# QKV row 4 turned by a transposing DMA, with row 3's turn and row 1's evictions rearranged

## The chip, the cores and the metric

The kernel runs on one core of one Trainium2 chip. The metric is the device time of one execution in microseconds; lower is better. The engines named below are TensorE (PE in the profile: matmuls, and PEld for its weight loads), VectorE (DVE), ScalarE (ACT), GpSimd (POOL) and SyncE (SP, which here only issues DMAs).

## What is computed

The input x has 2048 tokens of 576 numbers in bfloat16. A layer norm without weights gives xn. Two branches start from xn, and their sum goes onto x: local attention with 32 heads of 18, where each token looks at 8 earlier positions with a stride of 2, and a gated feed-forward block of width 4608.

```python
def _A_ref(x, wqkv, wo):
    H = 32; Dh = D // H
    W, dil = 8, 2
    qkv = (x @ wqkv).reshape(B, S, 3, H, Dh).transpose(2, 0, 3, 1, 4)
    q, k, v = qkv[0], qkv[1], qkv[2]
    idx = arange(S)[:, None] - (arange(W) * dil)[None, :]
    ...
    logits = jnp.einsum("bhsd,bhswd->bhsw", q, kg) * Dh ** -0.5
    logits = jnp.where(mask[None, None, :, :], logits, -1e9)
    attn = _softmax(logits, axis=-1)
    o = jnp.einsum("bhsw,bhswd->bhsd", attn, vg)
    return o.transpose(0, 2, 1, 3).reshape(B, S, D) @ wo
def _B_ref(x, w_gate, w_up, w_down):
    return (_silu(x @ w_gate) * (x @ w_up)) @ w_down
xn = _layernorm(x, axis=-1)
return x + _A_ref(xn, A_wqkv, A_wo) + _B_ref(xn, B_w_gate, B_w_up, B_w_down)
```

## The kernel before

**Rows and tiles.** The 2048 tokens are 16 "rows" of 128 tokens. Token 16p + r lies in partition p of row r. A row of xn has 576 columns and is padded to 640, so that it turns into five K tiles of 128. The last K tile holds columns 512 to 575 twice, in partitions 0 to 63 and 64 to 127.

**Stages.** First comes the QKV stage: each of the 16 rows is normalized, turned (its transposed form goes into `xnT`, since a matmul wants the contracted dimension in the partitions), multiplied by `wqkv` and evicted from PSUM. It ends near 59 us. Then follow four passes over 512 tokens each, with the feed-forward block on TensorE and the attention on VectorE beside it. The change lies in the first rows of the QKV stage.

**Order.** The schedule is written by hand: each engine gets its instructions in the order of the program text, and semaphores hold an instruction until its inputs are there. SP issues its DMAs in program order, and waits at each one for what it needs before it goes on to the next. PSUM has eight banks, which the pool `ps` deals in turn.

**A row on TensorE** (`p_row`, L321). The columns of the product are in four groups of 432, one PSUM bank each (`t[0]` to `t[3]`). The contraction is cut in halves of 64 partitions, and two matmuls, one for each half, run beside each other for two different groups: such a pair is the unit of the row. A row has 18 pairs: ten with `swap` 0 and eight with `swap` 1, where the halves change groups. Between the two a fence runs through a GpSimd no-operation (`fence_after`, L313), so GpSimd must be free when it is due. `between` is called after one K tile of `swap` 1, given by `at` as (pair of groups, K tile); there the next row is turned. Row 1 has its first K tile multiplied ahead (`u`).

**Turning a row.** Rows 0 and 1 are turned by `transp_pe`; rows 2, 3 and 4 by `transp_halves` (L274): ten matmuls of 64x64 against the identity, in five pairs, into two banks `pt`, which ScalarE and VectorE copy into `xnT` (L287). Rows from 5 on are turned by a transposing DMA from SP (`transp_dma`, L289), straight from the normalized row into `xnT`. Row 0 goes through `transp_dma` as well, but only for a use after the QKV stage.

**Normalizing a row.** `ln_stats` takes two halves of statistics (L214) and aggregates them (L218) on VectorE; `ln_sqrt` (L229) is on ScalarE; `normalize` (L467) takes the reciprocal (L234), applies it (L240) and fills the padding, for rows 0 and 1 with a GpSimd operation (L243) that reads the input, for the others with a VectorE copy (L246) of what L240 wrote. `ln_open(c)` makes the small tiles for rows 4c to 4c + 3.

**Evicting a row** (`p_evac`, L345). Six parts; `dve` lists those on VectorE, the others are on ScalarE. Parts 1 and 2 read `t[2]`, 3 and 4 read `t[1]`, part 0 reads `t[0]` and part 5 `t[3]`.

**DMAs of the stretch.** SP has issued by then, in this order, the inputs, the first gate and up weights (`load_gu(0)`), row 0's transposing DMA and two small fills of zeros (`wz`) into the rings `Kr` and `Vr`, 14 pieces of 1152 bytes each, all into partition 0. Rows 5 and later follow.

Of the kernel before, what the change touches and what calls it, by code (L numbers as in the profile page):

```python
# [70 lines left out]
def kernel(  # L71
# [124 lines left out]
    def new_ps(name):  # L196
        return ps.tile([P, 512], f32, name=name, tag="ps")
# [4 lines left out]
    def ln_open(c):  # L202
        mv = lns.tile([P, 4, 2], f32, name="mv")
        rstd = lns.tile([P, 4], f32, name="rstd")
        ln[c] = (xc_b[c], xn_b[c % 2], mv, rstd)
# [3 lines left out]
    def ln_half(r, k):  # L209
        c, j = divmod(r, 4)  # L210
        xc, xn, mv, rstd = ln[c]
        if k == 0:
            sums[r] = lns.tile([P, 2, 6], f32, name="stats")
        nc.vector.bn_stats(sums[r][:, k, :], xc[:, j, k * HALF:(k + 1) * HALF])  # L214

    def ln_aggr(r):
        c, j = divmod(r, 4)
        nc.vector.bn_aggr(ln[c][2][:, j, :], sums[r][:].rearrange("p c s -> p (c s)"))  # L218

    def ln_stats(r, n=1):  # L220
        for i in range(r, r + n):
            ln_half(i, 0)
            ln_half(i, 1)
            ln_aggr(i)

    def ln_sqrt(r, n=1):
        c, j = divmod(r, 4)
        xc, xn, mv, rstd = ln[c]
        nc.scalar.activation(rstd[:, j:j + n], mv[:, j:j + n, 1], ACT.Sqrt, bias=eps_t[:], scale=1.0)  # L229

    def ln_recip(r, n=1):
        c, j = divmod(r, 4)
        rstd = ln[c][3]
        nc.vector.reciprocal(rstd[:, j:j + n], rstd[:, j:j + n])  # L234

    def ln_apply(r):
        c, j = divmod(r, 4)
        xc, xn, mv, rstd = ln[c]
        dst = xn[:, j] if r else xn0
        nc.vector.tensor_scalar(dst[:, 0:D], xc[:, j], mv[:, j, 0:1], rstd[:, j:j + 1],  # L240
                                op0=ALU.subtract, op1=ALU.mult)
        if r < 2:
            nc.gpsimd.tensor_scalar(dst[:, D:DPAD], xc[:, j, 512:D], mv[:, j, 0:1], rstd[:, j:j + 1],  # L243
                                    op0=ALU.subtract, op1=ALU.mult)
        else:
            nc.vector.tensor_copy(dst[:, D:DPAD], dst[:, 512:D])  # L246
# [27 lines left out]
    def transp_halves(r):  # L274


        c, j = divmod(r, 4)
        xn = ln[c][1]
        pt = [new_ps("pt") for half in range(2)]
        for kt in range(KT):  # L280
            for half in range(2):
                rows = slice(64 * half, 64 * half + 64)
                nc.tensor.matmul(pt[half][:, kt * 64:(kt + 1) * 64], xn[rows, j, kt * P:(kt + 1) * P],  # L283
                                 ident[rows, rows], start=True, stop=True)
        for half, eng in enumerate((nc.scalar.copy, nc.vector.tensor_copy)):
            lo = r * P + 64 * half
            eng(xnT[:, :, lo:lo + 64], pt[half][:, 0:KT * 64].rearrange("p (k t) -> p k t", t=64))  # L287

    def transp_dma(r):  # L289
        c, j = divmod(r, 4)  # L290
        nc.sync.dma_start_transpose(xnT[:, :, r * P:(r + 1) * P], ln[c][1][:, j, :] if r else xn0)
# [7 lines left out]
    def p_mm(t, g, kt, half, r, start, stop):  # L299
        rows = slice(0, P) if half is None else slice(64 * half, 64 * half + 64)  # L300
        return nc.tensor.matmul(t[g][:, 0:G], xT_of(r)[rows, kt, :], w_at(g, kt, rows),  # L301
                                start=start, stop=stop)
# [10 lines left out]
    def fence_after(mm):  # L313
        f = nc.gpsimd.engine_nop()
        tc.add_manual_dep(f.ins, mm.ins.name, SYNC, reason="first half done")
        return f

    def fence_before(mm, f):
        tc.add_manual_dep(mm.ins, f.ins.name, SYNC, reason="banks change row tiles")

    def p_row(r, between=None, at=(0, 1), t=None):  # L321


        done = t is not None
        t = t or [None] * NG
        fence = {}
        for swap in range(2):
            for i in range(2):
                for kt in (0, 1, 2, 3) if swap else (0, 4, 1, 2, 3):
                    if done and kt == 0:  # L330
                        continue
                    for half in range(2):
                        g = i + 2 * (half ^ swap)
                        if t[g] is None:
                            t[g] = new_ps("qkv_ps")
                        mm = p_mm(t, g, kt, half, r, swap == 0 and kt == 0, swap == 1 and kt == 3)
                        if swap == 0 and kt == 3 and half == 1:
                            fence[i] = fence_after(mm)
                        if swap and kt == (1 if done else 0) and half == 0:
                            fence_before(mm, fence[i])  # L340
                    if swap and (i, kt) == at and between is not None:
                        between()
        return t

    def p_evac(r, t, only=range(6), between=None, last=6, dve=(5,)):  # L345


        c, j = divmod(r, 4)
        ks, vs = stage[2 * c % 4], stage[(2 * c + 1) % 4]
        vdst = vs[:, j, :].rearrange("p (d h) -> p d h", h=H)  # L350
        parts = [
            (QO[:, r, 0:G], t[0][:, 0:G]),
            (ks[:, j, HALF:D], t[2][:, 0:HALF]),
            (vdst[:, :, 0:8], t[2][:, HALF:G].rearrange("p (h d) -> p d h", d=DH)),
            (QO[:, r, G:D], t[1][:, 0:D - G]),
            (ks[:, j, 0:HALF], t[1][:, D - G:G]),
            (vdst[:, :, 8:H], t[3][:, 0:G].rearrange("p (h d) -> p d h", d=DH)),
        ]
        for n in only:
            if n == last:  # L360
                between()
            if r:
                (nc.vector.tensor_copy if n in dve else nc.scalar.copy)(*parts[n])  # L363
            elif n in dve:
                nc.vector.tensor_scalar(*parts[n], ln[0][3][:, 0:1], None, op0=ALU.mult)
            else:
                nc.scalar.mul(*parts[n], ln[0][3][:, 0:1])
# [24 lines left out]
    dve = Filler()  # L392
# [74 lines left out]
    def normalize(r, n=1):  # L467
        ln_recip(r, n)
        for i in range(r, r + n):
            ln_apply(i)  # L470
            if i > 4:
                transp_dma(i)

    def turn(r):
        return lambda: transp_halves(r)
# [15 lines left out]
    copy_pt(nc.scalar.copy, 0, (3, 4), pb[:, 2 * P:])  # L491
    ln_recip(0)
    ln_apply(0)
    ln_recip(1)
    ln_apply(1)

    t = [new_ps("qkv_ps") for g in range(NG)]
# [10 lines left out]
    u = [None] * NG  # L508
# [5 lines left out]
    ln_stats(2)  # L514
    ln_sqrt(2)
    normalize(2)
    p_evac(0, t, (5, 0, 3, 2, 4, 1), dve=(5, 2))
    ln_half(3, 0)
# [3 lines left out]

    p_row(1, turn(2), (0, 1), u)
    ln_aggr(3)
    p_evac(1, u, (0, 1, 2), dve=(1, 2))
    ln_sqrt(3)
    p_evac(1, u, (3, 4, 5), dve=())
    normalize(3)
    ln_open(1)
    ln_stats(4)  # L530
    for ring in (Kr, Vr):
        nc.sync.dma_start(ring[0:1, 0:HALO, :], wz[0:1, :].unsqueeze(1).to_broadcast([1, HALO, D]))

    t = p_row(2, turn(3))
    ln_stats(5)
    p_evac(2, t, (0, 1, 2), dve=())
    ln_sqrt(4, 2)
    p_evac(2, t, (3, 4, 5), dve=())
    normalize(4, 2)

    t = p_row(3, turn(4))
    ln_stats(6)
    p_evac(3, t, range(6), lambda: ln_sqrt(6), 4, ())
    normalize(6)
# [7 lines left out]
    for r in range(4, R):  # L552
        t = p_row(r)
# [92 lines left out]
    for tt in range(NTT):  # L646
# [28 lines left out]
        for sub in range(0, RT, 2):  # L675
            t, fence = {}, {}
# [36 lines left out]
```

## Time and profile before

| what | us |
|---|---|
| median of 3 runs | 503.44 (503.23 to 503.55) |
| the profiled execution, its own time | 503.32 |
| its span, first to last instruction | 501.5 |
| TensorE busy | 496.8 |
| VectorE busy | 329.0 |
| ScalarE busy | 200.6 |
| GpSimd busy | 2.6 |

The profile is of one execution. The span is what lies between its first and its last instruction; the time is 1.8 us longer. Times in the trace are counted from the start of the span. In lines of the order of time the first number is the start, the second the duration, then come the engine, the line, the operation, and what it writes and reads. SPq is SP issuing a DMA; "to landing" is the time from the start of the issue to the last completion. Several equal instructions in a row are merged into one line with their count, so the duration of such a line runs from the first start to the last end. Matmul durations overlap, since they are pipelined; what a matmul costs is seen from the start of the next one.

### The profile page before, as it was taken

How to read it: one execution, taken by the hardware profiler on the slowest of the kernel's cores; microseconds unless marked ns; L12 is line 12 of the kernel's file. 1: busy time of each engine (PE TensorE's matmuls, PEld its weight loads, DVE VectorE, ACT ScalarE, POOL GpSimd, SP SyncE). 2: the span in 40 equal slices, each digit the busy share in tenths (PEclk: the TensorE clock that was granted, in tenths of full speed). 3: DMA queues.
4: the chain of work that ended last, by engine and by line, in shares of the span. 5: the costliest groups of instructions: out<-in, count | busy, mean ns of one | idle time of the engine just before them, and what ended most of it. 6: DMA issues, size and time to landing. Idle time of an engine off the chain costs nothing.

```text
span 501.5 us, 13267 instructions
## 1 busy us (share of the span) xinstructions
PE 496.8 (99%) x5795; PEld 282.8 (56%) x5795; DVE 329.0 (66%) x478; ACT 200.6 (40%) x415; POOL 2.6 (1%) x9
## 2 busy tenths in 40 slices
PE   8999999999999999999999999999999999999997
PEld 4555544444677644444777544445777444446775
DVE  5889597998999698999897139995980222221001
ACT  4756657645300255544300445557000454553000
POOL 2000000000000000000000000000000000000000
PEclk9999999999999999999999999999999999999999
DMA  8689989898731045535631154453700335442200
GB/s 322 164 207 228 320 268 294 260 318 272 186 114 61 25 147 185 190 112 174 166 106 47 30 182 154 131 189 110 181 26 14 106 110 177 159 126 39 76 14 25
DMA packets 77186, 75.42 MB, mean 150 GB/s; under 512 B 22708, under 2 KB 72528, under 8 KB 77128
## 3 DMA queue, kind: packets, MB, share of 16 engines
q1 hardware_dynamic: 76840, 73.98, 49.2%
q8 instruction: 45, 0.74, 0.7%
q10 hardware_dynamic: 288, 0.59, 0.3%
q14 instruction: 13, 0.11, 0.1%
HBM read 58.76 MB, written 5.90 MB: 129 GB/s over the span
## 4 chain that ended last, share of the span: by engine, by line
PE 98%; DMA 1%; DVE 0%; SPq 0%; issue 0%
PE g_ps L600 56%; PE d_ps L629 32%; PE qkv_ps L301 11%; DMA hT<-in_A_wqkv_dram 1%; DVE ot L643 0%; PE pt L283 0%; SPq L145 0%; PE pt L262 0%; PE warm_ps L262 0%
## 5 line engine op out<-in xcount | busy, mean ns | idle before, releaser
L600 PE MATMUL g_ps<-xnT,gu 64*128 64x512 bf16 x2592 | 280.4, 376 | 0.0
L600 PEld LDWEIGHTS <-gu 64*128 64x128 bf16 x2592 | 126.1, 94 | 152.9
L611 ACT ACTIVATE sg<-g_ps 128x512 bf16<-128x512 f32 x144 | 87.3, 606 | 156.6 <-PE g_ps L600 156.6
L629 PE MATMUL d_ps<-wd,hT 64*128 64x288 bf16 x2304 | 146.4, 283 | 0.0
L629 PEld LDWEIGHTS <-hT 64*128 64x128 bf16 x2304 | 112.2, 94 | 29.7
L613 DVE TENSOR_TENSOR hT<-sg,uc 128x512 bf16<-128x512 bf16 x144 | 60.0, 419 | 93.9 <-ACT uc L612 93.8
L612 ACT CAST uc<-g_ps 128x512 bf16<-128x512 f32 x144 | 85.2, 592 | 0.0
L414 DVE TENSOR_REDUCE PP<-PP 128x64 f32<-128x1152 bf16 x64 | 84.9, 1346 | 0.4
L301 PE MATMUL qkv_ps<-hT,xnT 64*128 64x432 bf16 (+1 forms) x536 | 50.1, 343 | 0.0
L409 DVE TENSOR_TENSOR PP<-QO,Kr 128x2304 bf16<-128x2304 bf16 (+1 forms) x35 | 43.5, 1249 | 7.0 <-DMA Kr<-hT 6.8
L641 DVE TENSOR_TENSOR ot<-d_ps,xr 128x288 bf16<-128x288 f32 x30 | 12.3, 450 | 51.1 <-PE d_ps L629 51.1
L441 DVE TENSOR_TENSOR PP<-Vr,A 128x2304 bf16<-128x2304 bf16 (+1 forms) x35 | 43.2, 1250 | 0.4
L301 PEld LDWEIGHTS <-xnT 64*128 64x128 bf16 (+1 forms) x536 | 25.9, 94 | 22.5 <-ACT xnT L287 0.2
L446 DVE TENSOR_TENSOR PP<-PP 128x2304 bf16<-128x2304 bf16 x24 | 32.5, 1353 | 0.3
L611 ACT ACT_TABLE_LOAD x5 | 6.4, 1283 | 47.2 <-PE g_ps L600 47.2
L629 PE MATMUL d_ps<-wo,xnT 64*128 64x288 bf16 x288 | 22.9, 283 | 0.0
L363 ACT CAST hT<-qkv_ps 128x288 bf16<-128x288 f32 (+2 forms) x58 | 21.1, 427 | 0.5 <-ACT hT L363 0.5
L434 ACT ACTIVATE PP<-PP 128x1024 f32<-128x1024 f32 x4 | 4.2, 1056 | 31.2 <-DVE PP L430 31.2
L629 PEld LDWEIGHTS <-xnT 64*128 64x128 bf16 x288 | 14.0, 94 | 3.6
L643 ACT CAST ot<-d_ps 128x288 bf16<-128x288 f32 x1 | 0.4, 399 | 38.8 <-PE d_ps L629 38.8
L363 ACT CAST QO<-qkv_ps 128x432 bf16<-128x432 f32 (+1 forms) x30 | 12.3, 409 | 7.4 <-PE qkv_ps L301 7.4
L214 DVE BATCH_NORM_STATS2 stats<-wd 128x6 f32<-128x288 bf16 x32 | 12.9, 444 | 2.8 <-DMA wd<-in_A_x_dram 2.6
(53 smaller groups left out, 89.4 us busy)
## 6 DMA issues: line engine op xcount, KB each, us to landing
gu<-in_B_w_gate_dram SPq DMA_DIRECT2D x36, 512.0 KB, 3.9
gu<-in_B_w_up_dram SPq DMA_DIRECT2D x36, 512.0 KB, 5.2
wd<-in_B_w_down_dram SPq DMA_DIRECT2D x9, 576.0 KB, 6.4
kv_d<-hT SPq DMA_DIRECT2D x5, 576.0 KB, 6.0
gu<-in_B_w_gate_dram SPq DMA_DIRECT2D x36, 64.0 KB, 5.0
gu<-in_B_w_up_dram SPq DMA_DIRECT2D x36, 64.0 KB, 4.6
xr<-in_A_x_dram SPq DMA_DIRECT2D x8, 288.0 KB, 3.9
out_dram<-ot SPq DMA_DIRECT2D x16, 144.0 KB, 1.8
```

The source lines that it names most:

```text
L214: nc.vector.bn_stats(sums[r][:, k, :], xc[:, j, k * HALF:(k + 1) * HALF])
L301: return nc.tensor.matmul(t[g][:, 0:G], xT_of(r)[rows, kt, :], w_at(g, kt, rows), start=start, stop=stop)
L363: (nc.vector.tensor_copy if n in dve else nc.scalar.copy)(*parts[n])
L409: nc.vector.tensor_tensor(prod[:, a:b], QO[:, RT * tt + a:RT * tt + b, :], Kr[:, s:s + b - a, :], op=ALU.mult)
L414: nc.vector.tensor_reduce(L[:, w, rs], prod[:, rs].rearrange("p r (h d) -> p r h d", d=DH), axis=AX.X, op=ALU.add)
L441: nc.vector.tensor_tensor(dst[:, a:b], Vr[:, s:s + b - a, :].rearrange("p r (d h) -> p r d h", h=H), A[:, w, a:b].unsqueeze(2).to_broadcas ...
L446: nc.vector.tensor_tensor(dst, acc, pv, op=ALU.add)
L600: mm = nc.tensor.matmul(ring_ps[j][b][:], gu[rows, slot, k, fc], xnT[rows, kt, tok], start=(swap == 0 and kt == 0), stop=(swap == 1 and kt ...
L611: nc.scalar.activation(sg[:], t[0][:], ACT.Silu)
L612: nc.scalar.copy(uc[:], t[1][:])
L613: nc.vector.tensor_tensor(hT[:, ch * FC + j, :], sg[:], uc[:], op=ALU.mult)
L629: mm = nc.tensor.matmul(t[sub][h][:, 0:HALF], a[rows], w[rows, h * HALF:(h + 1) * HALF], start=(swap == 0 and n == 0), stop=(swap == 1 and ...
```

## The change

Row 4's turn on TensorE goes; `normalize(4)` issues a transposing DMA instead, as for the later rows. Row 4 is normalized alone and sooner: `ln_open(1)` and the first half of its statistics stand before row 1's evictions, the second half, the aggregate and the root behind `normalize(3)`, and `normalize(4)` right behind row 2's matmuls. Its padding is filled by GpSimd. Row 1's parts 1 and 2 are evicted by ScalarE, behind row 3's root. Row 3 is turned after K tile 0 of `swap` 1 of row 2, where it was K tile 1. Row 5 is then normalized alone too, with its root after part 3 of row 2's evictions.

```diff
@@ ln_apply
-        if r < 2:
+        if r in (0, 1, 4):
             nc.gpsimd.tensor_scalar(dst[:, D:DPAD], xc[:, j, 512:D], mv[:, j, 0:1], rstd[:, j:j + 1],
                                     op0=ALU.subtract, op1=ALU.mult)
@@ normalize
             ln_apply(i)
-            if i > 4:
+            if i > 3:
                 transp_dma(i)
@@ the first rows
     p_row(1, turn(2), (0, 1), u)
     ln_aggr(3)
-    p_evac(1, u, (0, 1, 2), dve=(1, 2))
+    ln_open(1)
+    ln_half(4, 0)
+    p_evac(1, u, (0,), dve=())
     ln_sqrt(3)
-    p_evac(1, u, (3, 4, 5), dve=())
+    p_evac(1, u, (2, 1, 3, 4, 5), dve=())
     normalize(3)
-    ln_open(1)
-    ln_stats(4)
+    ln_half(4, 1)
+    ln_aggr(4)
+    ln_sqrt(4)
     for ring in (Kr, Vr):
         nc.sync.dma_start(ring[0:1, 0:HALO, :], wz[0:1, :].unsqueeze(1).to_broadcast([1, HALO, D]))
 
-    t = p_row(2, turn(3))
+    t = p_row(2, turn(3), (0, 0))
+    normalize(4)
     ln_stats(5)
-    p_evac(2, t, (0, 1, 2), dve=())
-    ln_sqrt(4, 2)
-    p_evac(2, t, (3, 4, 5), dve=())
-    normalize(4, 2)
-
-    t = p_row(3, turn(4))
+    p_evac(2, t, (0, 1, 2, 3), dve=())
+    ln_sqrt(5)
+    p_evac(2, t, (4, 5), dve=())
+    normalize(5)
+
+    t = p_row(3)
     ln_stats(6)
     p_evac(3, t, range(6), lambda: ln_sqrt(6), 4, ())
     normalize(6)
```

## The prediction

> **What bounds the kernel now.** I read the page first, then what TensorE waits for, then the stretch from 10 to 24 us in order of time, then the DMA share by stretch and the landing times of single transposing DMAs. The page, its shares, chain and queues:
>
> ```profile
> span 501.5 us, 13267 instructions
> ...
> PE 496.8 (99%) x5795; PEld 282.8 (56%) x5795; DVE 329.0 (66%) x478; ACT 200.6 (40%) x415; POOL 2.6 (1%) x9
> ...
> q8 instruction: 45, 0.74, 0.7%
> ...
> PE 98%; DMA 1%; DVE 0%; SPq 0%; issue 0%
> ```
>
> All waits of TensorE over the whole span:
>
> ```profile
> PE warm_ps L174 <- PEq L697: 0.8, 1, 0.8
> PE pt L262 <- DVE wd L251: 0.7, 1, 0.7
> ```
>
> TensorE is the chain, and its only waits are over by 5.2 us. In the trace its matmuls then follow each other without a hole from 10.1 us to 498.1 us. So a microsecond is gained only by taking work from TensorE, and any new wait on it is paid in full. The stretch of the change, in order of time (start, duration, engine):
>
> ```profile
> 7.26 0.64 POOL L243 TENSOR_SCALAR wd<-wd,mv,rstd 128x64 bf16<-128x64 bf16 x1
> ...
> 11.35 1.44 SPq L291 DMA_TRANSPOSE xnT<-A  x1
> ...
> 12.84 1.03 SPq L532 DMA_DIRECT2D Kr<-ot  x1
> ...
> 13.91 0.82 SPq L532 DMA_DIRECT2D Vr<-ot  x1
> ...
> 15.40 0.31 PE L283 MATMUL pt<-ident,wd 64*128 64x64 bf16 x10
> ...
> 18.84 0.31 PE L283 MATMUL pt<-ident,wd 64*128 64x64 bf16 x10
> ...
> 18.98 21.33 PE L301 MATMUL qkv_ps<-hT,xnT 64*128 64x432 bf16 x232
> 19.03 6.25 SPq L291 DMA_TRANSPOSE xnT<-wd  x3
> ```
>
> DMA share (next to last column) by stretch:
>
> ```profile
> 13.30:17.80 4.50, 4.50 (x62) 2.46 (x60) 3.65 (x13) 3.13 (x12) 0.00 (x0) 1.00 1.13 313
> 17.80:20.10 2.30, 2.30 (x38) 1.28 (x36) 2.01 (x7) 1.58 (x5) 0.00 (x0) 1.00 0.01 1
> ```
>
> Issue to landing of the transposing DMAs of rows 0, 5 and 6, asked one by one:
>
> ```profile
> DMA to landing us min/median/max: 7.1/7.1/7.1
> ...
> DMA to landing us min/median/max: 2.6/2.6/2.6
> ...
> DMA to landing us min/median/max: 4.1/4.1/4.1
> ```
>
> Row 0's waited behind the gate and up weights, until 17.8; row 5's ran in an empty queue; why row 6's took 4.1 decides the case, see below.
>
> **The change, part by part.**
>
> *Row 4's turn leaves TensorE.* Ten 64x64 matmuls in five pairs: the next matmul starts at 18.98, they at 18.84, so 0.145 us (the 0.31 of the row is pipeline depth). This is the whole possible gain: **-0.145**.
>
> *Row 3's turn a K tile sooner* shifts it by one pair of matmuls. Between the turns of 15.40 and 18.84 lie 18 pairs and one turn: (3.44 - 0.145)/18 = 0.183 a pair. So it starts at 15.225. Its source is ready at 14.49 (pad copy of row 3, DVE). Cost 0.
>
> *Row 1's evictions to ScalarE.* DVE loses 0.40 + 0.30; ScalarE gains them, and two of its reads now end later. The pool deals eight banks in turn. The bank of row 1's third group goes to row 2's fourth group, whose first matmul starts at 14.13: ScalarE goes QO (12.90), root of row 3 (13.32), 18x8 (13.51), 288 (13.69 to 14.09), against 13.68 on DVE before. That is even; bounds 0 and 0.1, I take 0. Row 1's last group is read until 14.97; row 3's turn wants the bank at 15.225. Cost 0.
>
> *Row 4's statistics, apply and pad.* Statistics' first half goes at 13.06 into the hole before row 3's reciprocal (13.65), the second at 14.40 to 14.85, aggregate to 15.09, root on ScalarE 15.13 to 15.42. DVE turns to row 3's copy (15.60 to 16.09), reciprocal to 16.17, apply 16.21 to 16.64. The pad, a 0.18 copy on DVE, becomes a GpSimd operation of 0.64 to 0.74 (two rows of L243) from 16.27, beside the apply, as both rows did. It ends at 16.95; the last fence ahead of it on GpSimd passes at 15.27, the next one behind it is wanted at 17.79. Cost on TensorE's path 0, but it sets the issue.
>
> *One more transposing DMA on SP.* SP is past the two zero fills at 14.74, so it issues row 4's at **17.0** and is held 1.2 to 1.4 us; row 5's, next behind, comes at about 18.87 against 19.03, and is wanted at 23.2. Every later transposition on SP moves no later. Row 4 may start when row 3 ends: 20.08 before (18.98 plus six pairs), **19.93** after. So the change in time is the larger of -0.145 and (landing + 0.05 - 20.08), and waits ahead of that, as that for a bank, drown in it.
>
> *When does it land?* By row 5's 2.61: 19.6, and the wait is nil. But the packet records show a 16,384-byte packet of the instruction queue at 17.63 us that holds one DMA engine for 1026 ns: the last two packets of the zero fills on it start at 18.64 and 18.79, when the other 26 had started by 17.73. Row 6 shows what that does: a like packet, at 23.87 for 941 ns, came when nine of its 640 packets were left; these ran from 24.80 to 25.09, and all sixteen completions came at 25.92 to 26.02. A third, at 35.83, left some 30 packets of row 11's transposition, 27 ns apart; they ended at 37.59, and completions came at 38.25 to 38.44, while other engines' packets stood up to 1.29 us. So one late engine holds the transposition. TensorE's instructions up to 17.63 are the same in number, so I expect the fetch in the same place. Row 4's packets (first at 18.2) then start on that engine at 18.9; about 40 (640 over 16) by 23 to 27 ns end at 19.8 to 20.0; from the last packet to completion it took 0.35 (row 5), 0.66 and 0.83 (the two held ones). Landing 20.2 to 20.8; I take 20.55, between the held rows and the quiet one. Wait 0.67 from 19.93; net **+0.52**. As its start on that engine is set by the fetch, the issue could be 0.7 later for nothing.
>
> [...]
>
> The sum: -0.145 for the turn, +0.67 for the wait: +0.5 on the profiled execution's own 503.32 (its span 501.5 and 1.8 around it): **503.9**. The median of the runs shown is 503.44, 0.12 above that execution.
>
> **The rivals.**
>
> *The DMA is hidden.* The fetch falls on another engine or another time, or row 4's packets get past it. For it: 19.6 by row 5, and an idle queue (share 0.01). Against it: the zero fills' stragglers. Then -0.145, or -0.05 with the bank's wait: **503.2**.
>
> *Slower by over 0.2%.* The held transposition lands after 21.05, the point from which it decides (20.08 + 1.0). By row 6's whole 4.11 from 17.0 it lands at 21.1 and costs +1.1; by row 10's 4.95, held by the fetch of 35.83 too, at 21.95, +1.9: **504.4 to 505.2** (row 14's 5.39 ran among the stores of K and V and would give +2.4). For it: forty packets are late on that engine, not nine, and row 5's transposition comes right behind. Against: row 6's 4.11 holds 0.7 in which its packets had run before the fetch.
>
> *A bank is late.* ScalarE's chain slips by over 0.25 and row 3's turn waits for row 1's last group (15.0 against 15.2). Alone 503.3; behind row 4's wait nothing. I count it with the first rival.
>
> **How the numbers follow.** 0.2% is 1.0 us, about what a measurement of this kernel can tell from no change. The forecast (wait 0.3 to 1.1, so net +0.15 to +0.95) has 0.58, the hidden DMA 0.16, the late one 0.23, and 0.03 is left for a gain over 0.2%, for which I see no row, since TensorE loses just 0.145 of work. So faster 0.03, same 0.58 + 0.16 = 0.74, slower 0.23. Low end 503.1: the hidden case less part of the runs' spread of 0.3; high end 504.9, well into the late case, which leaves about 0.1 above.
>
> **What would show it.** Right: transposes gone at 18.84; row 4's first matmul at about 20.6, with TensorE waiting 0.7 for a DMA into xnT, the only new wait; that DMA issued at 17.0 with 3.5 to landing; an instruction packet at 17.6; after it every start moved by the same +0.5 to the end. Wrong: no such wait (row 4 at 19.93, landing under 3.0), a wait of over 1.2, an issue after 17.8, or a wait of TensorE on ScalarE near 14.1 or 15.2. Most likely to be wrong is the time from the held engine's last packet to completion.

## The result, and the profile after

The changed kernel takes 504.94 us in the median (503.89 to 507.60, twelve times) against 503.41 (503.19 to 503.81) of the kernel before on the same chip: the ratio of the two sets of times is 1.0036, its interval 1.0025 to 1.0047 (the ratio of the medians alone is 1.0030). It is slower, by 1.5 us where 0.5 was forecast. The twelve times lie in three groups: 503.89 to 504.49 (six), 505.40 to 505.67 (four), 507.47 and 507.60; the median lies in the gap between the first two. The profiled execution is one of the middle group, 505.40 by its own time, with a span 2.08 longer than before.

The page of the changed kernel: busy times, the instruction queue, the shares of the chain.

```profile
span 503.6 us, 13251 instructions
...
PE 497.6 (99%) x5785; PEld 283.5 (56%) x5785; DVE 328.0 (65%) x475; ACT 201.4 (40%) x417; POOL 3.4 (1%) x10
...
q8 instruction: 45, 0.74, 0.6%
...
PE 98%; DMA 1%; DVE 0%; issue 0%
```

Ten matmuls are gone, and 1% of the chain is now a DMA. All waits of TensorE (us in all, how often, the longest):

```profile
PE qkv_ps L301 <- DMA xnT<-wd: 1.8, 1, 1.8
PE warm_ps L174 <- PEq L701: 0.8, 1, 0.8
```

One new wait, of the kind forecast, 1.8 where 0.67 was forecast. The stretch in order of time:

```profile
15.13 0.29 ACT L229 ACTIVATE rstd<-mv,eps_t 128x1 f32<-128x1 f32 x1
15.23 0.31 PE L283 MATMUL pt<-ident,wd 64*128 64x64 bf16 x10
...
16.20 0.43 DVE L240 TENSOR_SCALAR wd<-wd,mv,rstd 128x576 bf16<-128x576 bf16 x1
16.27 0.73 POOL L243 TENSOR_SCALAR wd<-wd,mv,rstd 128x64 bf16<-128x64 bf16 x1 [8.50 <-DVE rstd L234]
...
17.02 2.07 SPq L291 DMA_TRANSPOSE xnT<-wd  x1
...
21.87 0.72 PE L301 MATMUL qkv_ps<-hT,xnT 64*128 64x432 bf16 x6 [1.77 <-DMA xnT<-wd]
```

Everything up to the issue of row 4's DMA, 17.02, came as forecast. Then row 4's first matmul starts at 21.87, where before it started at 20.08: +1.79, and the last matmul of the kernel starts 1.81 later (499.91 against 498.11). The other 0.27 of the 2.08 come behind it: from the start of the last matmul to the end of the span (the closing, below) are 3.70 us, before 3.43. Stretches of the same trace (the last three columns are the granted clock, the DMA share and GB/s):

```profile
17.80:20.10 2.30, 2.30 (x26) 1.02 (x22) 1.71 (x6) 1.50 (x5) 0.00 (x0) 1.00 1.15 55
19.76:21.87 2.11, 0.34 (x4) 0.00 (x1) 0.97 (x5) 1.76 (x7) 0.00 (x0) 1.00 1.02 101
21.87:25.50 3.63, 3.63 (x40) 1.97 (x42) 3.06 (x11) 1.12 (x4) 0.00 (x0) 1.00 0.35 69
```

From 17.80 to 20.10 the DMA share was 0.01 before and is 1.15 now, at 55 GB/s: packets are long under way and little is moved. The hole in TensorE is 2.11 from one start to the next, and the clock is 1.00 throughout. Issue to landing of row 0's DMA (issued at 11.32), then of row 4's:

```profile
DMA to landing us min/median/max: 9.6/9.6/9.6
```
```profile
DMA to landing us min/median/max: 4.8/4.8/4.8
```

Row 0's took 7.1 before. That is the first sign that the hold is not on row 4's packets alone. The packet records of the trace show it: 636 of row 0's 640 packets had started by 17.70, the other four come only after 18.2, and its completions came from 20.35 to 20.95. Of row 4's 640 packets, over a hundred had not started by 20.4, and no packet of either row started from 20.4 to 20.8; packets of row 4 stood up to 1.38 us.

### The profile page after: what moved, and what is told of

It reads as the page before. It is cut to its first block, busy times and chain, and to the rows that moved or that the text cites. A ratio compares the mean times of both kernels' runs of the same rounds, so it can differ in the third digit from the quotient of the medians.

```text
span 503.6 us, 13251 instructions
## 1 busy us (share of the span) xinstructions
PE 497.6 (99%) x5785; PEld 283.5 (56%) x5785; DVE 328.0 (65%) x475; ACT 201.4 (40%) x417; POOL 3.4 (1%) x10
## 4 chain that ended last, share of the span: by engine, by line
PE 98%; DMA 1%; DVE 0%; issue 0%
PE g_ps L604 56%; PE d_ps L633 32%; PE qkv_ps L301 10%; DMA xnT<-wd 1%; PE warm_ps L174 1%; PE pt L262 0%; DVE ot L647 0%; PE pt L283 0%; PE warm_ps L262 0%; PE warm_ps L177 0%
## 5 line engine op out<-in xcount | busy, mean ns | idle before, releaser
L363 ACT CAST hT<-qkv_ps 128x288 bf16<-128x288 f32 (+2 forms) x60 | 21.7, 428 | 0.0
```

## The experiments

The theory after this profile: TensorE's 16,384-byte instruction packet (here at 17.58 for 1.08 us, one of 45 in the trace; TensorE had begun 288 instructions by then, as it had at the packet of 17.63 in the trace of before) stands on one DMA engine and catches row 0's transposing DMA there, the two zero fills queue behind that, and row 4's DMA behind them, all completing in order; so row 4 lands a good 3 us after the packet's end. Rivals: the order of the queue alone delays row 4, and the packet is innocent; or the loss comes from the other edits (row 1's evictions, row 3's turn, the pad); and for the 0.27 at the end, the DMA added or ScalarE's added instructions shift what closes the kernel. The expectations name the theories by letters: A is the held engine (A' the same in the cleared queue; A'' where the full queue of the weights keeps that engine behind); B, C and Q are the queue without the packet (the fills, two transposing DMAs at once, the weights); D is the added DMA at the end, F and F' are ScalarE's instructions. Unless said otherwise an edit is made to the changed kernel; its medians and ratios are against the kernel before on the same chip, whose medians were 503.29 to 503.44.

**Zero fills behind row 7.**

```diff
@@ after ln_sqrt(4) -> after normalize(7)
-    for ring in (Kr, Vr):
-        nc.sync.dma_start(ring[0:1, 0:HALO, :], wz[0:1, :].unsqueeze(1).to_broadcast([1, HALO, D]))
...
     normalize(7)
+    for ring in (Kr, Vr):
+        nc.sync.dma_start(ring[0:1, 0:HALO, :], wz[0:1, :].unsqueeze(1).to_broadcast([1, HALO, D]))
```

> The changed kernel with one edit: the two zero fills are issued behind row 7's transposing DMA instead of ahead of row 4's. Theory A (a TensorE instruction packet of 16 KiB, near 17.6 us, holds one DMA engine for 1.0 us, and what the fills add on that engine is only their own 0.27 us): row 4 is still held, its DMA lands 20.2 to 21.5, TensorE waits 0.3 to 1.6, median 503.7 to 504.6, and the times stay as scattered as those of the changed kernel (503.9 to 507.6). Theory B (the 28 writes of the fills into one partition hold up the completion of what comes behind them): row 4's DMA lands by 20.0, TensorE waits under 0.1, median 503.2 to 503.4 with a scatter under 0.5.

504.88, ratio 1.0035 (1.0022 to 1.0048). Landing of row 4's DMA:

```profile
DMA to landing us min/median/max: 3.6/3.6/3.6
```

The packet came at 18.13, when row 0's DMA was nearly through: fifteen of its sixteen completions came by 18.92, the last one at 19.98, and row 4 landed at 20.88 instead of 21.83. The hole at row 4 is 0.89 instead of 2.11. The time did not follow, since the fills, in their new place, stand in front of row 8's DMA: issued at 30.57, it landed at 34.85, and TensorE has a hole of 1.00 at 33.89. Another 0.27 came ahead of the stretch, at the start of the kernel. Landing and wait are within theory A's ranges; the median is above its range, with the wait at row 8.

**Row 0's DMA behind row 7.**

```diff
@@ before row 1 -> after normalize(7)
     load_gu(0)
-    transp_dma(0)
...
     normalize(7)
+    transp_dma(0)
```

> The changed kernel with one edit: row 0's transposing DMA is issued behind row 7's instead of ahead of the zero fills. Theory A: the weights and fills are through before or near 17.6, the held engine has nothing of a transposing DMA cut in two when the packet comes, row 4 starts on it at about 18.7: landing 20.0 to 20.5, wait 0.1 to 0.6, median 503.4 to 503.9, and the upper groups of times (above 505) are gone. Theory B: the fills are still right ahead of row 4, so it lands after 20.8 and the median stays at 504.2 or more. Theory C (two transposing DMAs in flight, row 0's and row 4's, get in each other's way): median 503.2 to 503.5.

503.99, ratio 1.0013 (1.0004 to 1.0022). The packet (17.06 to 18.33) now caught the last weights (19.42), the fills completed by 19.60 and 19.77, and row 4:

```profile
DMA to landing us min/median/max: 3.2/3.2/3.2
```

landed at 20.11, with a hole of 0.49 left. Of the two single moves, this one gives more back: it is 0.70 above the kernel before, where the changed kernel is 1.53. All eleven times lie from 503.38 to 504.43: the groups above 505 are gone, as theory A expected of a kernel in which row 0's DMA can't be caught.

**Both.** The edits of the two runs before, together.

```diff
@@ before row 1 -> after normalize(7)
-    transp_dma(0)
...
-    for ring in (Kr, Vr):
-        nc.sync.dma_start(ring[0:1, 0:HALO, :], wz[0:1, :].unsqueeze(1).to_broadcast([1, HALO, D]))
...
     normalize(7)
+    for ring in (Kr, Vr):
+        nc.sync.dma_start(ring[0:1, 0:HALO, :], wz[0:1, :].unsqueeze(1).to_broadcast([1, HALO, D]))
+    transp_dma(0)
```

> The changed kernel with both: the zero fills and row 0's transposing DMA behind row 7's. Row 4's DMA is the first behind the weights. Theory A: the instruction packet near 17.6 still holds one engine until 18.65, row 4 runs on it from there: landing 19.9 to 20.3, wait 0 to 0.4, median 503.3 to 503.7. Theories B and C: it lands at 19.6 (17.0 + 2.6), no wait, median 503.27 (the kernel before, 503.41, less the 0.145 of the turn).

505.51, ratio 1.0049 (1.0035 to 1.0063). Row 4's DMA landed at 19.70 and TensorE doesn't wait for it. All the waits of TensorE for DMAs into `xnT` are at rows behind:

```profile
PE qkv_ps L301 <- DMA xnT<-wd: 1.8, 2, 1.6
```

They are at 32.84 (a hole of 1.96, row 8) and 41.20 (0.51): three small DMAs more on SP and in the queue ahead of row 8's. The wait was moved, not removed; the part of the expectation on row 4 held, the one on the time did not.

**Row 4 turned by TensorE, the rest of the change kept.**

```diff
-            if i > 3:
+            if i > 4:
                 transp_dma(i)
...
-    t = p_row(3)
+    t = p_row(3, turn(4))
```

> The changed kernel with one part undone: row 4 is turned by TensorE's ten matmuls between row 3's, as before, and no transposing DMA of row 4 is issued; row 1's evictions on ScalarE, the pad on GpSimd, the sooner statistics and row 3's sooner turn stay. All theories on the DMA: no wait of TensorE after 10 us, median 503.41 as before, within 0.15. If instead the moved evictions or the pad cost something of their own, it stays above 503.7 and TensorE shows a wait on ScalarE near 14.1 or 15.2.

504.14, ratio 1.0018 (1.0009 to 1.0026). There is no wait of TensorE behind 10.5 us, so the whole wait belongs to row 4's DMA. But the time is 0.85 above before, not even with it: the start of the QKV stage is 0.34 later in the profiled execution, and from the last matmul to the end are 4.28 us. The last store's issue to landing, in this run and then in the changed kernel:

```profile
DMA to landing us min/median/max: 2.6/2.6/2.6
```
```profile
DMA to landing us min/median/max: 1.7/1.7/1.7
```

An 8,192-byte instruction packet at 500.25, for 0.71 us, lay in the store's time. In the changed kernel it comes at 504.21, after the end of the work.

**The closing: one DMA more in the kernel before.**

```diff
@@ the kernel before
-    for c in range(1, 4):
+    for c in range(1, 3):
         nc.sync.dma_start(xc_b[c], x_v[:, 4 * c:4 * c + 4, :])
+    for i in (0, 2):
+        nc.sync.dma_start(xc_b[3][:, i:i + 2, :], x_v[:, 12 + i:14 + i, :])
```

> The kernel before with one edit: the load of x rows 12 to 15 goes as two DMAs, so there is one DMA more, as in the changed kernel, and every later DMA moves to the next completion semaphore. Theory D (the last store's semaphore is then waited for in the middle of SP's closing list, not at its end, and the closing costs 0.27 us more): median 0.2 to 0.3 above the kernel before, TensorE without a new wait, last matmul to end of span 3.65 instead of 3.38. Rival: a DMA more costs nothing at the end (the 0.27 of the changed kernel came from elsewhere): median within 0.1.

503.48, ratio 1.0002 (0.9993 to 1.0011); the closing is 3.43 as before. Theory D's 0.27 is not there. Its smaller part is: SP waits for the last store in the middle of its list of closing semaphores, as in the changed kernel, and needs two more steps behind it; but here the store also landed 0.1 sooner after the last matmul (2.47 us behind it, before 2.58), so the two cancel. The trace has a second use: with row 4 still on TensorE, the packet came at 17.35 and row 0's DMA landed at 20.23, where the profile of before had 17.63 and 18.42.

**A clear queue: fills ahead of the weights, row 0's DMA late, as many DMAs as before.**

```diff
-    for c in range(1, 4):
-        nc.sync.dma_start(xc_b[c], x_v[:, 4 * c:4 * c + 4, :])
+    nc.sync.dma_start(xc_b[1], x_v[:, 4:8, :])
+    nc.sync.dma_start(wdf[:, 2 * XC:4 * XC].rearrange("p (r d) -> p r d", d=D), x_v[:, 8:16, :])
...
+    for ring in (Kr, Vr):
+        nc.sync.dma_start(ring[0:1, 0:HALO, :], wz[0:1, :].unsqueeze(1).to_broadcast([1, HALO, D]))
     load_gu(0)
-    transp_dma(0)
...
-    for ring in (Kr, Vr):
-        nc.sync.dma_start(ring[0:1, 0:HALO, :], wz[0:1, :].unsqueeze(1).to_broadcast([1, HALO, D]))
...
             if r == 4:
                 move(0, ms=(2,))
+            if r == 5:
+                transp_dma(0)
```

> The changed kernel with the queue ahead of row 4's DMA cleared: the zero fills are issued ahead of the gate and up weights, row 0's transposing DMA behind row 11's, and x rows 8 to 15 come in one DMA, so that there are as many DMAs as in the kernel before. All theories on the queue: row 4's DMA lands 19.6 to 19.9, no wait of TensorE after 10.2 us, tail 3.38, median 0.1 to 0.2 below the kernel before (the 0.145 of the turn). If row 4 is still late or another row waits, the median is 0.2 or more above it and something other than the fills, row 0's DMA and the closing list is at work.

504.18, ratio 1.0018 (1.0009 to 1.0026). Nothing is left between the weights and row 4's DMA, and it still is late:

```profile
DMA to landing us min/median/max: 3.4/3.4/3.4
```

It landed at 20.62, 1.61 after the packet's end (17.77 to 19.01), with a hole of 0.72. That missed what all theories expected of this kernel (19.6 to 19.9). The order of fills and row 0's DMA has no cause for that wait; the packet has, and the weights just ahead were still a rival. The rest of the loss is 0.19 at the start of the stage and a closing of 3.61.

**The packet moved by the warm-up.** The number of warm-up matmuls sets how many of TensorE's instructions lie before a point in time.

```diff
-    warm_pe(10, 1)
+    warm_pe(6, 1)     # the first kernel
+    warm_pe(6, 17)    # the second
```

> The changed kernel with warm_pe(6, 1) for warm_pe(10, 1): four warm-up matmuls, so eight TensorE instructions fewer, and its instruction packet near 17.6 us comes about 0.4 us later. Theory A (it is this packet that cuts row 0's transposing DMA in two in the slower groups of runs): row 0's DMA and the fills are through before it in every run, the packet only delays the start of row 4 on one engine: landing 20.4 to 20.9, wait 0.5 to 0.9, all runs 503.9 to 504.5 (0.27 of it the closing list), none above 505. Theory B or C (fills, or row 0's DMA, by themselves): the same three groups as the changed kernel, 503.9 to 507.6.

505.08, ratio 1.0036 (1.0024 to 1.0048). Inconclusive: in the profiled execution the granted clock was 0.50 from 7.12 to 10.53 us, behind the shorter warm-up, and the stage started 1.6 us late, which moved row 4's issue as well (18.63). The other four executions have no such clock in their mean (0.999 and 1.000, against 0.995), and no trace was kept of them. There is no wait near row 4, whose DMA landed in 2.62, with row 0's already in at 18.63.

> The changed kernel with warm_pe(6, 17) for warm_pe(10, 1): the same warm-up time in more and smaller matmuls, 24 TensorE instructions more, and the instruction packet near 17.6 us comes about 1.1 us sooner. Theory A: the packet falls into the weights, one engine runs a microsecond late through row 0's DMA and the fills, so row 0's DMA is still open when row 4's starts: landing 21 or later, wait over 1, all runs 505 or more. Theory B or C: the same three groups as the changed kernel, or less if a late engine does not matter.

506.40, ratio 1.0057 (1.0040 to 1.0074); six times from 504.53 to 507.65, the profiled one 507.10. The packet came at 17.09, only half a microsecond sooner; the weights' last landing went from 17.90 to 19.39, and row 0's, the fills' and row 4's landings (20.98, 21.22, 21.62, 21.85) stayed where they were. One of the six times is below the 505 that theory A set as the lowest. The stretches of the hole and of the slow clock behind it:

```profile
19.60:21.90 2.30, 0.34 (x6) 0.01 (x2) 1.16 (x6) 1.76 (x7) 0.00 (x0) 1.00 1.16 102
21.90:25.70 3.80, 3.80 (x24) 1.70 (x26) 3.17 (x11) 0.29 (x1) 0.00 (x0) 0.56 0.43 85
22.36:25.78 3.42, 3.42 (x24) 1.42 (x22) 2.74 (x10) 0.29 (x1) 0.00 (x0) 0.50 0.49 96
```

Behind a hole of 2.30 the granted clock is 0.56 over 3.8 us, and in them 0.50 for 3.4 us, and a pair of matmuls takes 0.35 instead of 0.18. That costs 3.42 x 0.50 = 1.7 us, and this time of 507.1 is 1.7 above the profiled one of the changed kernel, whose hole of 2.11 left the clock at 1.00.

**The packet sooner by far, in the clear queue**, and then the same with row 1's parts 1 and 2 back on VectorE.

```diff
@@ the clear queue, and
-    warm_pe(10, 1)
+    warm_pe(0, 41)
@@ the second kernel also
-    p_evac(1, u, (0,), dve=())
+    p_evac(1, u, (0, 1, 2), dve=(1, 2))
     ln_sqrt(3)
-    p_evac(1, u, (2, 1, 3, 4, 5), dve=())
+    p_evac(1, u, (3, 4, 5), dve=())
     normalize(3)
-    ln_half(4, 1)
-    ln_aggr(4)
+    ln_open(1)
+    ln_stats(4)
     ln_sqrt(4)
```

> The cleared queue (zero fills ahead of the gate and up weights, row 0's transposing DMA behind row 11's, as many DMAs as before) with warm_pe(0, 41) for warm_pe(10, 1): the same warm-up time in 41 small matmuls, so TensorE is 60 instructions further and asks for its instruction packet up to 2.7 us sooner. Theory A' (what holds row 4 is the instruction packet alone; a transposing DMA that it catches completes 1.6 to 1.8 us after the packet's end): the packet starts before 16.8, row 4 lands before 19.9, TensorE has no wait after 10.8, median 503.2 to 503.6, up to 0.2 of that a slower closing as in the changed kernel. Theory Q (the weights ahead in the queue hold row 4, and the packet only came along): landing 20.4 or later and median 504.0 or more, as with the cleared queue and warm_pe(10, 1).

503.76, ratio 1.0007 (0.9998 to 1.0016). The packet came at 13.74, four microseconds sooner, and row 4 still landed at 20.42, with a hole of 0.84. The weights fill the queue from 9 to 17.7 us (the DMA share over it is 1.08 in the traces of before and after), and the completions of the last weights came from 18.03 to 19.68. Theory A' missed (20.42 where under 19.9 was expected), and the landing is the one that theory Q named, though the median is below Q's 504.0. What theory A'' makes of it, that the engine which lost 1.25 us to the packet stays behind as long as the queue is full, fits the spread of the weights' completions; the trace does not name the engines.

> The cleared queue with the sooner instruction packet, and row 1's second group evicted by VectorE as in the kernel before, so that ScalarE has as many instructions as there (415). Row 4 is turned by a DMA, row 3 a K tile sooner. Theories A' and F together: no wait of TensorE after 10.8, closing 3.4, median 0.1 to 0.2 below the kernel before (the 0.145 of the turn). If it stays above the kernel before, a cost is left that neither names.

503.99, ratio 1.0010 (1.0001 to 1.0018). Row 4 landed at 19.88, a hole of 0.30, and the closing was 3.31, the shortest of all. But a gate weight came late, 55 us on:

```profile
PE g_ps L602 <- DMA gu<-in_B_w_gate_dram: 1.0, 1, 1.0
```

No gain over the kernel before, where 0.1 to 0.2 was expected.

**ScalarE's count.** Two, three or seven small activations more at the start of the kernel before.

```diff
@@ the kernel before
-    nc.scalar.activation(warm[:], eps_t[:], ACT.Sqrt)
+    for i in range(3):    # 4 and 8 in the other two
+        nc.scalar.activation(warm[:], eps_t[:], ACT.Sqrt)
```

> The kernel before with two more instructions on ScalarE (the warm-up activation issued three times), as many as the changed kernel has (417). Theory F: the packet is not yet in the last store but one engine's closing drain waits for it: last matmul to end 3.5 to 3.7, median 0.1 to 0.25 above the kernel before. Rival: closing 3.4, median within 0.1.

> The kernel before with three more instructions on ScalarE: the warm-up activation on one number is issued four times at the start, where ScalarE is idle. It has then as many ScalarE instructions as the changed kernel with row 4 turned by TensorE (418). Theory F (that kernel's 0.8 us came from ScalarE's instruction packet of 8 KiB, which its three more instructions pull into the last store): an 8,192-byte packet 1.5 to 2.2 us behind the last matmul, the last store lands near 2.6 us instead of 1.74, last matmul to end 4.2 to 4.3 instead of 3.4, median 503.9 to 504.3. Rival (the 0.8 us came from that kernel's other edits): median within 0.2 of the kernel before.

> The kernel before with seven more warm-up activations on ScalarE (415 + 7). Theory F' (the last 8,192-byte instruction packet is ScalarE's and moves to an earlier instruction as the count grows; 415 to 417 closed in 3.43, 418 in 3.59): the packet comes within 2.2 us of the last matmul, into the last store, closing 4.0 or more, median 503.9 to 504.4. Rival (the closing has nothing to do with ScalarE's count): closing 3.4 to 3.6, median 503.4 to 503.6.

503.51 (ratio 1.0001, 0.9992 to 1.0010), 503.58 (1.0003, 0.9994 to 1.0012) and 503.41 (1.0000, 0.9992 to 1.0009), with closings of 3.42, 3.59 and 3.42. No median differs clear of noise, though the first kernel has as many ScalarE instructions as the changed one (417) and the second as many as the run with row 4 turned by TensorE (418). The number of ScalarE's instructions alone does not decide the end: 417 and 422 left it as it was. But the second's closing is 0.16 longer, and in the same place as in the changed kernel: ScalarE's last closing instruction but one (a drain) starts 3.25 us behind the last matmul and takes 0.127, in the changed kernel 3.36 and 0.127, in the kernel before 2.98 and 0.014.

**The weights behind row 5, and behind row 8**: an empty queue for row 4.

```diff
     ln_half(3, 1)
-    load_gu(0)
     transp_dma(0)
...
     normalize(5)
+    load_gu(0)        # the first kernel
...
+        if r == 8:        # the second
+            load_gu(0)
```

> The changed kernel with one edit: the first gate and up weights (1.15 MB) are issued behind row 5's transposing DMA instead of ahead of row 0's. Theory A'' (the instruction packet puts one DMA engine about a microsecond behind, and since the weights keep the queue full, that engine stays behind until they are through, so what comes next in the queue completes late): with the queue drained at 14.5, row 0's DMA and the fills are through by 17, row 4's DMA lands before 20.0 in nearly every run and TensorE waits under 0.1 for row 4; the weights may make a later row late, so the median may be anything from 503.3 to 505, but the profile shows no wait of TensorE near 20. Rival (a transposing DMA issued at 17.0 is late whatever the queue, by what is already in flight on its own): landing 20.3 or later, wait 0.4 or more near 20.

505.37, ratio 1.0039 (1.0027 to 1.0051). The packet came at 14.69, row 0's DMA was done by 15.30, and row 4's:

```profile
DMA to landing us min/median/max: 2.6/2.6/2.6
```

landed at 19.69; TensorE doesn't wait for it. A wait of the same size came at the next place where a row's DMA stands behind the weights, row 6:

```profile
26.38:28.49 2.11, 0.34 (x4) 0.00 (x1) 1.97 (x8) 1.70 (x6) 0.00 (x0) 1.00 0.53 120
```

The gain of the change can be read here without the wait: from the start of the stage's head (10.58, before 10.52) to a matmul of row 5 (26.02, before 26.10) are 15.440 us instead of 15.585: 0.145 less, as worked out.

Whether the packet is innocent can be read off row 6, whose DMA's packets start when weights, fills and the earlier rows have landed. In nine of the traces it was issued at 21.66 to 22.25 and a packet came at 23.55 to 24.13, while it was in flight; in five it was issued at 21.55 to 21.99 and the packet came at 24.32 or later. Issue to landing is 4.02 to 4.63 in the nine and 2.55 to 2.57 in the five. (The other four differ: weights ahead of it; a later issue; and two with a packet at 21.7 or 21.8, over or nearly over before row 6's own packets, with 2.60 and 2.95.) The longest of the nine (both moves, packet 24.07 to 25.19) and the changed kernel (packet 26.14):

```profile
DMA to landing us min/median/max: 4.6/4.6/4.6
```
```profile
DMA to landing us min/median/max: 2.6/2.6/2.6
```

So the packet makes a transposing DMA late with nothing ahead of it in the queue.

> The changed kernel with the first gate and up weights issued in the turn of row 8, just ahead of the second ones, behind every transposing DMA of the stage. Theory A'': row 4 lands before 20.0, no wait of TensorE in the QKV stage; median 503.2 to 503.6 if the attention's K and V moves, now behind the weights, still come in time, with the closing costing up to 0.27. Rival: row 4 late as before, 504 or more.

505.60, ratio 1.0046 (1.0032 to 1.0059). Row 4 landed in 2.60 again, and no transposing DMA was waited for in the whole QKV stage. The weights themselves were late now:

```profile
PE g_ps L605 <- DMA gu<-in_B_w_up_dram: 0.6, 1, 0.6
PE g_ps L605 <- ACT sg L616: 0.4, 1, 0.4
```

Holes of 0.96 at 74.9, 0.73 at 91.4 and 0.48 at 92.1 cost more than row 4's wait saved.

**Row 4 turned by TensorE, and row 1's parts 1 and 2 evicted by VectorE**; the sooner statistics, the pad on GpSimd and row 3's sooner turn stay.

```diff
@@ the kernel with row 4 turned by TensorE, and
-    p_evac(1, u, (0,), dve=())
+    p_evac(1, u, (0, 1, 2), dve=(1, 2))
     ln_sqrt(3)
-    p_evac(1, u, (2, 1, 3, 4, 5), dve=())
+    p_evac(1, u, (3, 4, 5), dve=())
```

> The changed kernel with row 4 turned by TensorE and row 1's second group evicted by VectorE as in the kernel before: what stays of the change is row 4's sooner statistics, its GpSimd pad and row 3's sooner turn; ScalarE has two instructions fewer (416) than where it evicts. Theory F': the packet leaves the last store, closing 3.4 to 3.6, median 503.3 to 503.6. Rival (the pad or the order costs, not the count): closing 4.2 and median 504.0 or more, as where ScalarE evicts.

503.31, ratio 0.9998 (0.9989 to 1.0006): no difference from before. The page of this run:

```profile
span 501.7 us, 13273 instructions
...
PE 497.4 (99%) x5795; PEld 283.0 (56%) x5795; DVE 328.9 (66%) x478; ACT 200.8 (40%) x416; POOL 3.4 (1%) x10
```

So the other rearrangements cost nothing that can be measured, and the 0.85 of the run with row 4 on TensorE went with the two evictions on ScalarE. Theory F' named this run's closing rightly (3.42), but its reason, ScalarE's count, missed with the seven activations, so the reason stays open.

**The landings side by side.** Left out are the kernel with three activations, the later packet, the two with the packet sooner by far and the weights behind row 8. The packet is TensorE's 16,384-byte packet nearest to the stretch, from its start to its end; the other columns are the last completion of each DMA, in us from the start of the span, as the traces have them. "Ahead" and "behind" are where an edit moved the DMA out of the way.

| kernel | packet | last weights | row 0 | fills | row 4 |
|---|---|---|---|---|---|
| before | 17.63-18.66 | 17.89 | 18.42 | 19.83, 20.04 | TensorE |
| before, one DMA more | 17.35-18.71 | 19.70 | 20.23 | 21.36, 21.59 | TensorE |
| before, 2 activations | 17.42-18.48 | 19.39 | 19.93 | 20.51, 21.12 | TensorE |
| before, 7 activations | 17.46-18.65 | 19.50 | 20.02 | 21.03, 21.25 | TensorE |
| row 4 on TensorE, DVE | 17.50-18.94 | 19.84 | 20.26 | 21.45, 21.66 | TensorE |
| row 4 on TensorE | 18.26-19.33 | 18.52 | 20.41 | 20.58, 20.88 | TensorE |
| after | 17.58-18.66 | 17.90 | 20.95 | 21.21, 21.61 | 21.83 |
| packet sooner | 17.09-18.23 | 19.39 | 20.98 | 21.22, 21.62 | 21.85 |
| fills behind | 18.13-19.19 | 18.29 | 19.98 | behind | 20.88 |
| clear queue | 17.77-19.01 | 18.68 | behind | ahead | 20.62 |
| row 0 behind | 17.06-18.33 | 19.42 | behind | 19.60, 19.77 | 20.11 |
| both behind | 16.96-18.11 | 19.31 | behind | behind | 19.70 |
| weights behind row 5 | 14.69-15.96 | behind | 15.30 | 15.93, 16.46 | 19.69 |

Down the table, one of the DMAs in flight at the packet completes late, and what is queued behind it follows in order. Whether it is the weights, row 0's DMA or only one count of a fill (in the trace of before the last of 14, at 19.83) seems to hang on some 0.1 us in the packet's time: with 17.63 before and 17.58 after, row 0's DMA landed at 18.42 and at 20.95.

## Why the prediction was wrong

**Right: the bound and the gain.** TensorE sets the end, every new wait on it was paid in full (+1.79 at row 4's first matmul, +1.81 at the last), and the turn is worth 0.145, as the run with the weights behind row 5 shows.

**Right: everything up to the issue.** Row 3's turn at 15.23 (15.225 forecast), the pad from 16.27 to 17.00 (to 16.95), the issue at 17.02 (17.0). No wait for a bank and none on ScalarE. SP was held 2.07 instead of 1.2 to 1.4; row 5's issue, at 19.20 instead of 18.87, still landed in time.

**Right in kind: the mechanism.** The packet came at 17.58 (17.6 forecast), it took 1.08, and the transposing DMA landed late behind it. That it holds one DMA engine is read from the few packets left behind it (four of row 0's 640); the trace does not name the engines. The run with a clear queue shows this part alone, 20.62 against the forecast's 20.55. That it is so close is in part luck: its packet ended at 19.01 where 18.66 was forecast, and the DMA landed 1.61 behind that, not 1.89. The times agree: 503.8 to 504.2 is where the kernels lie whose only hole is of 0.5 to 0.9. The short group of the changed kernel's own times, 503.89 to 504.49, may be such executions; no profile of one was taken, so that is an inference.

**Wrong: the landing of row 4 (20.2 to 20.8).** The step that failed is "Row 4's packets (first at 18.2) then start on that engine at 18.9": it puts nothing but the fills' two last packets ahead of row 4's on the held engine, and takes row 0's transposition for landed, as it was at 18.42 in the one trace of before. In the profiled execution the packet came 50 ns sooner against that queue, row 0's transposition was still in flight, with four of its packets not started, and landed at 20.95, the two fills at 21.21 and 21.61, and row 4 at 21.83. The term of 0.67 measured 1.93 (the hole of 2.11 less the 0.18 of an ordinary pair). The time from the last packet to completion, named as the most likely to be wrong, was not what failed: row 4's packets ran until about 21.0 instead of 19.8 to 20.0, and its counts came 0.6 to 0.9 later, where 0.35 to 0.83 had been read. That this is the commoner case could not be seen in the profile of before, but can be seen now: in six other executions in which TensorE still turned row 4, row 0's DMA landed at 19.93 to 20.41 (five are in the table; the sixth, with three activations, had 20.34), and the fills at 20.5 to 21.7. The profile of before showed the uncommon queue, one of seven, and the sum was made from it. The slow rival's bound, +1.1 to +1.9 by the rows of 4.11 and 4.95, held the case (4.80, +1.79); its chance of 0.23 was too small. It argued with the number of packets on the held engine, not with what stands ahead of them.

TensorE itself shows no wait for these packets behind the warm-up: its only wait on its sequencer, 0.8 us, lies there, in a trace with 45 of them. For other traffic the packet had a cost: holes of 0.3 to 2.3 us in TensorE stood behind it, in the kernels where a DMA that was needed soon was in flight with it or queued behind one that was. The completion counts of one DMA came apart in some cases: in the profile of before, 13 of the 14 counts of a fill came by 18.88 and one at 19.83, and of row 7's transposition in the changed kernel fifteen came by 26.56 and one at 28.20, behind a packet of 26.14 to 27.12. Row 0's transposition in the changed kernel was different: with four packets held, all sixteen counts were late, from 20.35 to 20.95. With two packets held, in the run with row 4 on TensorE, fifteen of its counts came by 18.92 and one at 20.41, so what decides between the two is open.

**Wrong: "every start moved by the same amount to the end".** That holds to the last matmul, but the closing took 0.27 more, a term that the sum did not have. What was found: the two pairs of runs that differ chiefly in row 1's two evictions have closings of 4.28 and 3.42 (row 4 on TensorE), and 3.61 and 3.31 (the packet sooner by far), longer with ScalarE each time. The trace of the changed kernel divides the 0.27: SP's closing list ends 0.09 later, since the last store's semaphore stands in its middle (the run with one DMA more has that too, and made up for it by an earlier store), and 0.18 is ScalarE's drain, which starts 3.36 us behind the last matmul instead of 2.98. The same late drain is in the kernel before with three activations more (closing 3.59), not with two or seven. Why the evictions' place or three activations make that drain late stays open. The 0.85 of the run with row 4 on TensorE is another thing, the last store's landing at 2.6 instead of 1.7.

**Not foreseen: the clock.** The two times near 507.5 match the profiled one of the run with the packet half a microsecond sooner, where a hole of 2.30 was followed by 3.4 us at a clock of 0.50. No trace was taken of these two, but the mean granted clock of each execution is on record: 0.996 and 0.997 for these two, 0.999 to 1.000 for the other ten, and 3.4 us at half clock lower the mean over 505 us by 0.0034. The median of 504.94 falls between the first two groups, 0.04 above the range's high end, which was set within the late case with none of these additions; the six executions below 504.5 lie inside the range, so on which side of its end the median falls hangs on how many of the executions were late ones.

No version tried beats the kernel before. Without the wait there are 0.145 us to win, and each way of making row 4's landing safe (fills, row 0's DMA or weights elsewhere) put one of those in front of another DMA that TensorE needs.

## What to carry to other kernels

In these runs a few packets held back made a whole transposing DMA late (four of row 0's 640, and it landed in 9.6 us instead of 7.1), so before a matmul is made to wait for one, look at what stands ahead of it (instruction packets and earlier transpositions too), not at the mean DMA share, which was 0.01 in that stretch of the kernel before. A landing time read from one profile is a sample: where some 0.1 us in the arrival of a packet seems to decide which transfer is caught (row 0's landings of 18.42 and 20.95), take the late case for the likely one until a second trace says otherwise. Work worth 0.145 us is not worth a transfer whose landing varies by 2 us.

## What the runs showed of the hardware that was not expected

An instruction packet of 16,384 bytes took 0.88 to 2.00 us in these traces (1.03 to 1.48 near the stretch). In a queue filled by 8 us of weights, a packet at 13.74 was followed by the last weights at 19.68, 1.65 after the first of their completions, as if an engine held by the packet did not catch up; the trace does not name the engines.

A transposing DMA of 128x640 landed in 2.55 to 2.62 us in an empty queue with no packet in its time. With a packet in its time and no other unfinished transposition ahead it landed in 3.2 to 4.7 us, 1.1 to 3.1 after the packet's end (25.19 to 26.29, 19.01 to 20.62, 18.33 to 20.11, 25.35 to 28.45), and 3.2 to 3.6 after it with another transposition and two small fills between (18.66 to 21.83, 18.23 to 21.85).

A hole in TensorE of 2.30 us (with 0.34 of pipelined matmul in it) was followed by 3.42 us at a clock of 0.50, from 22.36 to 25.78; one of 2.11, in two kernels, was not. No run tested what tells the two apart.
